# Delta-rule attention and an MLP on one core: join products on four 32x32 tiles, state updates with 48 stationary columns, and another planned order

## The chip, the cores and the metric

The kernel runs on one core of a Trainium2 chip. The metric is the time of one execution on the device in microseconds (us); lower is better. TensorE (PE in the profile) multiplies, VectorE (DVE), ScalarE (ACT) and GpSimd (POOL) work element by element, and SyncE (SP) issues most of the transfers.

## The reference

Two blocks follow each other, all in float32. The first is a linear attention with the delta rule: 4 x 8 heads, 768 tokens, 48 values a head, and a state of 48x48 for each head.

```python
k_n = k / (np.linalg.norm(k, axis=-1, keepdims=True) + 1e-06)
state = np.zeros((B, H, D, D))
for t in range(S):
    y[:, :, t] = q[:, :, t] @ state                       # before the update
    v_old = state^T k_n[t]
    state = state + beta[t] * outer(k_n[t], v[t] - v_old)
```

The result is laid out as (4, 768, 384) and goes through a layer norm and an MLP with a residual:

```python
xn = (x - mean) / sqrt(var + 1e-6) * g_ln
out = x + relu(xn @ w_ch1) @ w_ch2                        # 384 -> 1536 -> 384
```

## The kernel before

**Tiling.** The tokens are worked in 12 chunks of 64 (C), all 32 heads of a chunk at once. Two chunks form a slab. The step by step recurrence within a chunk is replaced by the inverse of a triangular matrix of 64x64 for each head, X, built from the gram matrix of the keys. Its two diagonal blocks of 32 rows (BK) come from `rows_inverse`: for a slab, 31 rows, each with a product (L1051, into tmp) and a subtraction (L1058, into xb) on VectorE, every one of which depends on the one before. The blocks then go through memory (xb to xd to xt). The block below the diagonal is made by `join` from two groups of products: e = gram block times the first diagonal block (L1118), then z = the second diagonal block times e (L1123). Each group has 32 products of 32x32, for 16 heads in each of two partition halves. `blocks_join` does the same a level lower, for chunk 1 alone, whose inverse is built from blocks of 16.

**One chunk on TensorE** then takes these small groups of 32 products each, named here as in the prediction: the gram matrices (L967, kt only), P (queries times keys, L967 with qt), e and z (the join), ks (state times keys, L1168 into two), qs (state times queries, L1168 into by), u (L1223), y (L1230, the chunk's output) and the state update s (L1240). Between them stand other engines: v minus ks on VectorE (L1175), the copy of u on ScalarE (L1225), s added to s_all on VectorE (L1250), the masked P on VectorE (L998), and for the join a transpose on VectorE (L1111) and evictions on ScalarE (L1128 into es, L1133 into xt). A small product is placed in the array by the partitions of its operands: the rows by where they are read, the columns by where the output lies. `quad(n)` is the n-th strip of 32 partitions, `half(n)` the n-th of 64.

**The MLP** works on the 256 tokens that a chunk has over the 4 batches. Chunks 0 to 2 have a plain first layer (L1495), the others one with eleven products instead of twelve (L1428); the second layer is plain for chunk 0 (L1517) and has seven products instead of eight for the others (L1596). It reads its normed input xnt some way behind y: copy, statistics, scaling, transposing, partly through memory.

**The order.** The code does not fix the order by itself. Each step (a group of products, one element-wise operation, one transfer) is handed to `Line.add` with an assumed cost, its dependencies and a priority. `Line.schedule` runs a planner: it works backwards from due times, then forwards with the assumed costs, and picks for each engine what starts next. The steps are then emitted in order of planned start, and every engine executes its own list in that order, transfers of SP and ACT in one common order. So a step that waits holds all that stands behind it on its engine. The numbers that steer the planner are HOP (time from a step to a dependent one on another engine), 0.03 us for a dependent step on the same engine, PASS (a small product's half, 0.0165 us), the lists DUE and CAP (due times of the MLPs and of single steps), and URGENT (how far a small group may go ahead of MLP work). Where TensorE would wait long, the planner inserts products of zeros (L1674) that keep its clock up.

Of the kernel before, what the change touches and what calls it, by code (L numbers as in the profile page):

```python
# [74 lines left out]
class Line:  # L75
# [3 lines left out]
    HOP, GIVE, PATIENCE, SLACK, EAGER = 0.17, 0.1, 0.8, 3.0, 0.068  # L79
# [132 lines left out]
    def offer(self, u):  # L212
        t = u.t0
        for d in u.deps:
            t = max(t, d.end + (0.03 if d.eng == u.eng and d.bulk is None else self.HOP))
        u.ready = t + u.lag
        self.avail[u.eng].append((u.ready, u))

    def foresee(self, now):

        soon, ends = {e: [] for e in ENGS}, {}
        for s in self.held:
# [5 lines left out]
            for d in s.deps:  # L228
                z = d.end if d.end is not None else ends.get(d, max(now, self.free[d.eng]) + d.cost)
                t = max(t, z + (0.03 if d.eng == s.eng and d.bulk is None else self.HOP))  # L230
# [129 lines left out]
    def schedule(self):  # L360
# [5 lines left out]
        for s in reversed(every):  # L366
            took = s.cost if s.bulk is None else s.cost + self.DMA_ISSUE + self.DMA_DONE + 2 * s.bulk
            took = max(took, 0.031 * s.np if s.due is None else 0.0)
            late = [u.pr - took - (0.03 if u.eng == s.eng else self.HOP) for u in users[s]]
# [32 lines left out]
def kernel(  # L402
# [129 lines left out]
    ATT = FK[2]  # L532
    hp_e = ((0, 0), (1, 1), (0, 1), (1, 0))
# [223 lines left out]
    def pe(n, fn, r, w, arr=0.0, **kw):  # L757
        return add("PE", n * PASS, fn, r, w, np=n, arr=arr, **kw)
# [312 lines left out]
    def blocks_join(c, **kw):  # L1071
# [5 lines left out]
        XN, ES = ([(n, 0), (n, 1)] for n in ("xn", "es"))  # L1077
# [14 lines left out]
        pe(128, prod_e, gk + XN, ATT, 0.22, **kw)  # L1092
        add("ACT", act(512), lambda: nc.scalar.mul(es, pe_, -1.0), ATT, ES, **kw)
        pe(128, prod_z, ES + xq + XT, BY[:2], 0.22, **kw)
# [6 lines left out]
    def xt_keys(c):  # L1101
        return [("xq", c % NX, n) for n in range(8)] + [("xz", c % NX)] + [
            (n, c % NX, g) for n in ("xt", "xo") for g in range(2)
        ]

    def join(c, **kw):
# [8 lines left out]
        def prod_e():  # L1115
            for h in range(GH):
                for e in range(2):
                    nc.tensor.matmul(p[quad(2 * e + 1), h], gs[quad(2 * e), h, BK:C], xnj[quad(2 * e), h])  # L1118

        def prod_z():  # L1120
            for h in range(GH):
                for e in range(2):
                    nc.tensor.matmul(p[quad(2 * e), h], es[quad(2 * e + 1), h], xt[quad(2 * e + 1), h, c0 : c0 + BK])  # L1123

        pe(64, prod_e, gk + [("xn", 0), ("xn", 1)], [ATT[1]], 0.11, name=f"e{c}", **kw)
        for e in range(2):
            rows = quad(2 * e + 1)
            add("ACT", act(512), lambda rows=rows: nc.scalar.mul(es[rows], p[rows], -1.0), [ATT[1]], [("es", e)], **kw)  # L1128
        pe(64, prod_z, [("es", 0), ("es", 1)] + xq, [ATT[0]], 0.11, name=f"z{c}", **kw)
        for e in range(2):  # L1130
            rows = quad(2 * e)
            add(
# [684 lines left out]
```

## Time and profile before

| | us |
|---|---|
| median of 3 runs | 560.88 |
| runs | 559.5 to 561.1 |
| span of the profiled execution | 559.2 |
| TensorE busy in it | 527.6 |
| VectorE busy | 365.0 |
| GpSimd busy | 252.5 |
| ScalarE busy | 193.1 |

The profiled execution has its span as its own time, from the first to the last instruction; what the device time has around it is not in the trace, and the median of the runs lies 1.7 us above that span. An engine's busy time does not hold the issue of transfers. TensorE's matmuls overlap, so groups of them are compared from their start to the next start.

### The profile page before, as it was taken

How to read it: one execution, taken by the hardware profiler on the slowest of the kernel's cores; microseconds unless marked ns; L12 is line 12 of the kernel's file. 1: busy time of each engine (PE TensorE's matmuls, PEld its weight loads, DVE VectorE, ACT ScalarE, POOL GpSimd, SP SyncE). 2: the span in 40 equal slices, each digit the busy share in tenths (PEclk: the TensorE clock that was granted, in tenths of full speed). 3: DMA queues.
4: the chain of work that ended last, by engine and by line, in shares of the span. 5: the costliest groups of instructions: out<-in, count | busy, mean ns of one | idle time of the engine just before them, and what ended most of it. 6: DMA issues, size and time to landing. Idle time of an engine off the chain costs nothing. (4 is left out here: it accounts for less than half of the span.)

```text
span 559.2 us, 23067 instructions
## 1 busy us (share of the span) xinstructions
PE 527.6 (94%) x10052; PEld 479.9 (86%) x10052; DVE 365.0 (65%) x884; ACT 193.1 (35%) x452; POOL 252.5 (45%) x399
## 2 busy tenths in 40 slices
PE   7778979999959999999999998999999999999996
PEld 4667857689848899998999988999999999999996
DVE  6775459870898833898957886758979336253331
ACT  5786733232222324322403314404412225323030
POOL 5362428319863565375363314361353602426243
PEclk9897989999989999999999999999999999999999
DMA  9884883579344677544525255652523410111101
GB/s 170 277 156 127 210 207 53 83 195 119 64 74 65 153 161 98 108 87 96 112 52 91 46 111 111 133 111 58 115 38 83 106 30 32 31 35 53 28 1 29
DMA packets 195973, 54.67 MB, mean 98 GB/s; under 512 B 186136, under 2 KB 189344, under 8 KB 195872
## 3 DMA queue, kind: packets, MB, share of 16 engines
q1 hardware_dynamic: 190112, 40.39, 37.4%
q10 hardware_dynamic: 3552, 9.63, 5.3%
q0 software_dynamic: 2208, 3.17, 3.6%
q8 instruction: 79, 1.29, 1.0%
q14 instruction: 22, 0.18, 0.1%
HBM read 36.38 MB, written 16.78 MB: 95 GB/s over the span
## 5 line engine op out<-in xcount | busy, mean ns | idle before, releaser
L1596 PE MATMUL f<-w_sb,h_all 128*128 128x192 f32 x396 | 95.0, 330 | 0.0
L1582 POOL TENSOR_TENSOR h_all<-h_all 128x256 f32<-128x256 f32 x99 | 72.9, 739 | 48.2 <-PE f L1596 41.9
L1596 PE MATMUL f<-words,h_all 128*128 128x192 f32 x396 | 91.2, 329 | 0.1
L1428 PE MATMUL f<-xnt,w_sb 128*128 128x128 f32 x648 | 89.2, 277 | 0.0
L1621 POOL TENSOR_TENSOR words<-h_all 128x128 f32<-128x128 f32 x66 | 30.4, 473 | 123.6 <-ACT h_all L1447 105.3
L1428 PEld LDWEIGHTS f<-xnt,w_sb 128*128 128x128 f32 x648 | 81.0, 192 | 0.8
L1450 DVE TENSOR_TENSOR h_all<-f,h_all 128x256 f32<-128x256 f32 x135 | 56.4, 420 | 34.6 <-PE f L1428 22.9
L1058 DVE TENSOR_TENSOR xb<-xb,tmp 128x60 f32<-128x60 f32 (+19 forms) x170 | 71.8, 423 | 3.3
L1051 DVE TENSOR_TENSOR tmp<-xb,gb 128x60 f32<-128x60 f32 (+19 forms) x170 | 68.8, 405 | 3.8 <-DVE gb L1041 0.5
L1596 PEld LDWEIGHTS f<-words,h_all 128*128 128x128 f32 x396 | 67.9, 190 | 0.9 <-issue 0.2
L1596 PEld LDWEIGHTS f<-w_sb,h_all 128*128 128x128 f32 x396 | 66.4, 190 | 1.2 <-issue 0.2
L1495 PE MATMUL f<-xnt,w_sb 128*128 128x256 f32 x216 | 52.3, 394 | 2.6 <-ACT h_all L1504 2.6
L1495 PEld LDWEIGHTS f<-xnt,w_sb 128*128 128x128 f32 x216 | 41.0, 195 | 10.6 <-ACT h_all L1504 3.5
L559 POOL DMA_DIRECT2D tb<-in_k_dram x64 | 42.0, 661 | 11.8 <-DVE kt L947 11.4
L1614 DVE TENSOR_TENSOR o<-f,x 128x192 f32<-128x192 f32 x33 | 11.7, 355 | 53.2 <-PE f L1596 42.5
L1447 ACT ACTIVATE h_all<-f 128x256 f32<-128x256 f32 x54 | 20.6, 382 | 55.8 <-PE f L1428 33.7
L1596 PE MATMUL f<-w_sb,words 128*128 128x192 f32 x132 | 32.8, 332 | 1.2 <-DVE o L1614 1.2
L1504 ACT ACTIVATE h_all<-f 128x256 f32<-128x256 f32 x36 | 13.6, 381 | 40.2 <-PE f L1495 32.5
L1447 ACT ACTIVATE h_all<-h_all 128x256 f32<-128x256 f32 x54 | 22.1, 413 | 12.8 <-DVE h_all L1450 12.5
L1614 POOL TENSOR_TENSOR o<-o,words 128x192 f32<-128x192 f32 x22 | 13.1, 613 | 25.9 <-DVE words L1614 25.9
L1596 PEld LDWEIGHTS f<-w_sb,words 128*128 128x128 f32 x132 | 22.5, 190 | 1.8 <-DVE o L1614 1.5
L1444 ACT COPY h_all<-f 128x256 f32<-128x256 f32 x27 | 10.0, 372 | 36.9 <-PE f L1428 36.8
(235 smaller groups left out, 936.5 us busy)
## 6 DMA issues: line engine op xcount, KB each, us to landing
words<-in_moe_w_ch_dram ACTq DMA_DIRECT2D x10, 768.0 KB, 5.5
gd<-gsb SPq DMA_DIRECT2D x11, 512.0 KB, 4.9
v<-in_v_dram SPq DMA_DIRECT2D x24, 192.0 KB, 3.6
out_dram<-o SPq DMA_DIRECT2D x48, 96.0 KB, 2.3
kr<-in_k_dram SPq DMA_DIRECT2D x46, 96.0 KB, 3.1
xld<-xlt SPq DMA_DIRECT2D x9, 384.0 KB, 2.6
xnt<-xld SPq DMA_DIRECT2D x36, 96.0 KB, 2.7
gb<-gd SPq DMA_DIRECT2D x40, 64.0 KB, 3.1
```

The source lines that it names most:

```text
L559: add(eng, cost, lambda: QUEUE[eng].dma_start(out=out_, in_=in_), r, w, bulk=n * ns / 16e3, **kw)
L1051: lambda j=j, n=n, w=w, t=t: nc.vector.tensor_tensor(out=t, in0=xv[:, 0:n, j : j + 1].to_broadcast([128, n, w]), in1=gv[:, j : j + 1, j + ...
L1058: "DVE", dve(n * w), lambda t=t, rest=rest: nc.vector.tensor_tensor(out=rest, in0=rest, in1=t, op=ALU.subtract),
L1428: nc.tensor.matmul(wide(p[:, 128 * n : 128 * n + 128]), w[:, f : f + 128], r, start=start and n == 0, stop=stop, skip_group_check=True)
L1447: add("ACT", act(256), lambda: nc.scalar.activation(to[0], p, ACTF.Relu), pk, to[1])
L1450: add("DVE", dve(256), lambda: nc.vector.tensor_tensor(out=to[0], in0=ps(p), in1=y[0], op=op), [*pk, *y[1]], to[1])
L1495: nc.tensor.matmul(p[:, 0:TOK], w1_sb[:, t, f * 128 : (f + 1) * 128], xnt[:, t], start=(t == 0), stop=(t == KC - 1))
L1504: lambda hk=hk, p=p: nc.scalar.activation(h_all[:, hk] if c <= LNPE else h_all[:, hk].rearrange("p (g i b) -> p i g b", g=2, b=BK), p[:, 0 ...
L1582: add(eng, cost, lambda: e.tensor_tensor(out=out_, in0=x, in1=y, op=op), r, w, port=2 if eng == "Pool" else 1, pr=-2)
L1596: lambda f=f, t=start and f == 0: nc.tensor.matmul(p[:, 0:D2], lhs(f), rhs[:, f], start=t, stop=(f == F2 - 1), skip_group_check=True),
L1614: lambda: e.tensor_tensor(out=out_, in0=a, in1=b_, op=ALU.add), r, w, pr=pr,
L1621: lambda f=f + i: e.tensor_tensor(out=s3[f], in0=one(0, 0)[0](f), in1=one(1, 0)[0](f), op=ALU.subtract),
```

## The change

- In `join`, the 32 products of e and of z are placed on four 32x32 tiles in turn instead of two: heads of even and odd number now write different column strips. They read the same two row strips as before. Each eviction of 32 partitions x 512 elements becomes two of 32 x 256, one for each parity of head.
- In `state_up`, the stationary side has 48 columns (D) instead of 64 (DP, of which 16 are zeros) in all chunks but the first. s_all is written in 112 partitions instead of 128.
- In the planner, join products, the products of `blocks_join` and state updates have lower assumed costs (0.0097 and 0.0135 us for half a product), a dependent step of the same engine may start at once (NEXT = 0.0 instead of 0.03), and DUE, CAP and with them URGENT have other values. The planned order of all engines differs in consequence. The same 5,059 products are issued on TensorE, 22 of them products of zeros as before.

```diff
-    HOP, GIVE, PATIENCE, SLACK, EAGER = 0.17, 0.1, 0.8, 3.0, 0.068
+    HOP, NEXT, GIVE, PATIENCE, SLACK, EAGER = 0.17, 0.0, 0.1, 0.8, 3.0, 0.068
...
-            t = max(t, d.end + (0.03 if d.eng == u.eng and d.bulk is None else self.HOP))
+            t = max(t, d.end + (self.NEXT if d.eng == u.eng and d.bulk is None else self.HOP))
...
+    SROWS = slice(0, DP + D)
...
-    def pe(n, fn, r, w, arr=0.0, **kw):
-        return add("PE", n * PASS, fn, r, w, np=n, arr=arr, **kw)
+    def pe(n, fn, r, w, arr=0.0, per=PASS, **kw):
+        return add("PE", n * per, fn, r, w, np=n, arr=arr, **kw)
...
         def prod_e():
-            for h in range(GH):
-                for e in range(2):
-                    nc.tensor.matmul(p[quad(2 * e + 1), h], gs[quad(2 * e), h, BK:C], xnj[quad(2 * e), h])
+            for j in range(GP):
+                for hp, e in hp_e:
+                    h = 2 * j + hp
+                    nc.tensor.matmul(p[quad(2 * e + 1 - hp), h], gs[quad(2 * e), h, BK:C], xnj[quad(2 * e), h])
 
         def prod_z():
-            for h in range(GH):
-                for e in range(2):
-                    nc.tensor.matmul(p[quad(2 * e), h], es[quad(2 * e + 1), h], xt[quad(2 * e + 1), h, c0 : c0 + BK])
...
+            for j in range(GP):
+                for hp, e in hp_e:
+                    h = 2 * j + hp
+                    nc.tensor.matmul(p[quad(2 * e + hp), h], es[quad(2 * e + 1), h], xt[quad(2 * e + 1), h, c0 : c0 + BK])
+
+        pe(64, prod_e, gk + [("xn", 0), ("xn", 1)], ATT, 0.11, per=0.0097, name=f"e{c}", **kw)
+        for hp, e in hp_e:
+            o, i = es[quad(2 * e + 1), hp::2], p[quad(2 * e + 1 - hp), hp::2]
+            add("ACT", act(256), lambda o=o, i=i: nc.scalar.mul(o, i, -1.0), ATT, [("es", e, hp)], **kw)
...
         def state_up():
-            p_s = p_2
+            p_s, w = p_2, D if c else DP
...
-                        p_s[half(hp), e, j], kp[half(e ^ hp), h0 * DP : h0 * DP + DP], us[half(e ^ hp), h0]
+                        p_s[DP * hp : DP * hp + w, e, j], kp[half(e ^ hp), h0 * DP : h0 * DP + w], us[half(e ^ hp), h0]
...
-                add("DVE", dve(768), lambda: nc.vector.tensor_tensor(out=s_all, in0=s_all, in1=p_2, op=ALU.add), TWO, ["s_all"], **kw)
+                add("DVE", dve(768), lambda: nc.vector.tensor_tensor(out=s_all[SROWS], in0=s_all[SROWS], in1=p_2[SROWS], op=ALU.add), TWO, ["s_all"], **kw)
...
-    DUE = [48.277, 71.818, 105.201, 129.927, 160.904, 198.354, 225.618, 268.079, 296.41, 349.475, 397.211, 414.674, 2.36, 1.205, 1.444, 27.102]
-    CAP = [80.445, 120.608, 203.575, 297.613, 389.16, 84.616, 102.629, 154.396, 189.571, 211.797, 265.167, 306.93, 344.143, 373.749, 426.77]
+    DUE = [50.992, 114.068, 314.926, 205.564, 149.356, 477.876, 478.934, 312.28, 346.185, 350.453, 686.787, 470.901, 1.129, 0.014, 0.752, 73.348]
+    CAP = [205.235, 241.575, 287.664, 628.512, 352.468, 284.041, 97.509, 453.871, 237.917, 199.779, 306.658, 413.158, 502.3, 617.624, 487.101]
```

33 lines of the change are left out of this document (13 added, 20 removed).

## The prediction

> **What bounds the kernel now.** I read the page first (busy times, slices, chain), then the busy times by stretch, then the order of events on TensorE and VectorE in the stretch that is not full. Times are us from the start of the span. A product shows as two records, so a group of 32 small products is "x64".
>
> ```profile
> span 559.2 us, 23067 instructions
> ...
> PE 527.6 (94%) x10052; PEld 479.9 (86%) x10052; DVE 365.0 (65%) x884; ACT 193.1 (35%) x452; POOL 252.5 (45%) x399
> ...
> PEclk9897989999989999999999999999999999999999
> ...
> PE 39%; ACT 0%; DVE 0%; issue 0%; DVEq 0%
> ```
>
> TensorE is busy for 94%, the chain that ended last consists of TensorE work alone for its last 39% (217 us), and the granted clock is full but for a few early slices. The next view, busy time of each engine by stretch, tells where the other 32 us are.
>
> ```profile
> core 0: us, PE busy (x) PEld busy (x) DVE busy (x) ACT busy (x) POOL busy (x), PEclk, DMA share, GB/s
> ...
> 60.00:100.00 40.00, 35.87 (x834) 27.32 (x836) 26.91 (x56) 17.29 (x31) 22.76 (x28) 0.96 0.63 133
> ...
> 150.00:175.00 25.00, 18.27 (x515) 15.34 (x508) 23.27 (x39) 7.71 (x19) 13.19 (x17) 0.86 0.51 79
> 175.00:555.00 380.00, 375.98 (x6769) 357.94 (x6767) 244.81 (x586) 113.68 (x276) 164.91 (x272) 1.00 0.38 78
> ```
>
> From 175 on TensorE is busy for 376 of 380 us: there each us of TensorE work taken away is a us of the time. From 150 to 175 it is busy for 18.3 of 25 us at clock 0.86, and part of that is products of zeros that only keep the clock up. So there are two places for a gain: less TensorE work after 175, and an order that has no hole before it.
>
> **The two new product shapes.** TensorE's events in order of time; the columns are start, length, engine, line, shapes, count:
>
> ```profile
> 79.00 1.29 PE L1085 MATMUL f<-xnj,gsb 32*32 32x32 f32 x128
> 80.21 1.56 PE L1495 MATMUL f<-xnt,w_sb 128*128 128x256 f32 x6
> ...
> 376.30 1.20 PE L1118 MATMUL by<-xnj,gsb 32*32 32x32 f32 x64
> 377.43 0.59 PE L1596 MATMUL f<-w_sb,h_all 128*128 128x192 f32 x2
> ...
> 391.81 1.11 PE L1240 MATMUL two<-u,kr 64*64 64x48 f32 x64
> 392.85 1.16 PE L1428 MATMUL f<-xnt,w_sb 128*128 128x128 f32 x8
> ```
>
> From start to the next start, a join product on two 32x32 tiles takes 1.13 us for 64 passes, and blocks_join on four tiles 1.21 us for 128. About 0.1 us of each is the change to and from another shape (my estimate: the difference between a lone small group and one that follows another). So a pass costs 16 ns on two tiles and 8.7 on four, 32 to 35 ns for each tile either way: what counts is how many tiles take turns. On four tiles a join product should cost 64 x 8.7 ns + 0.1 = 0.66 us and save 0.47. Bounds: 0.52, if the whole 1.21 halves, and nothing, if four tiles that share two row strips do not overlap as the four of blocks_join do, which lie in four row strips. I take 0.47, because the state update (four tiles on two row strips, 64 stationary columns) runs at (1.04 - 0.1) / 64 = 14.7 ns a pass, 29 ns for each strip, less than the 32 ns that a strip takes now for half the columns; a strip that served one tile at a time could not do that. There are 22 such products (11 chunks, two each), 16 of them after 175: 7.5 us there.
>
> A rule of the Trainium skill speaks against this edit: "TensorE: Matmul & The Clock Gate", Part 3 (Packing small matmuls), says that a weight load overlaps running products only where the row group differs. By it the join products would stay at 1.13 us, since the row strips are two before and after. The state update's 29 ns speaks against the rule here, but in another tile size, so it is a rival below.
>
> The state update loads 48 stationary columns in place of 64. The weight loads by column count, and the evictions that change, from the groups of instructions:
>
> ```profile
> L1428 PEld LDWEIGHTS f<-xnt,w_sb 128*128 128x128 f32 x648 | 81.0, 192 | 0.8
> ...
> L1240 PEld LDWEIGHTS two<-u,kr 64*64 64x64 f32 x704 | 11.7, 135 | 2.0 <-issue 1.9
> ...
> L1118 PEld LDWEIGHTS by<-xnj,gsb 32*32 32x32 f32 x384 | 6.5, 108 | 0.9 <-ACT rstd L1280 0.2 <-issue 0.2
> ...
> L1128 ACT ACTIVATE es<-by 32x512 f32<-32x512 f32 x12 | 7.1, 589 | 16.1 <-PE by L1118 16.0
> ...
> L877 ACT COPY xt<-by 64x256 f32<-64x256 f32 (+1 forms) x9 | 3.3, 366 | 0.8 <-ACT h_all L742 0.7
> ```
>
> The load grows by 0.85 ns a column (108, 135, 192), and a tile's pass is 32 ns at 32 columns and 59 at 64, so I put 48 columns at the middle, 45.5: 16 x 45.5 ns + 0.1 = 0.83 us instead of 1.04, 0.21 saved (between nothing, if the 48 moving columns set the pace, and 0.26, if it falls in proportion). Ten updates, eight after 175: 1.7 us. With the joins 9.2 us after 175.
>
> What it adds: each join eviction becomes four of 32x256 for two of 32x512, 4 x 366 - 2 x 589 = 0.29 us more ScalarE for each product, 6.4 us on an engine that is busy for 35%. On the path it lengthens product to product by 0.29 us; in the changed order at least 3 us of TensorE work stand between e and z and between z and u, against about 1.7 needed, so I cost it at nothing. The 48 rows of s_all change no element count.
>
> **The order.** The planner's smaller step between dependents, its new due times and costs give another order from the start. TensorE, VectorE and SyncE around the hole:
>
> ```profile
> 95.04 0.68 PE L1187 MATMUL two<-v,xt 32*64 32x48 f32 x32
> ...
> 99.34 1.15 PE L1230 MATMUL by<-u,pt 64*64 64x48 f32 x64
> ...
> 105.33 3.39 PE L1517 MATMUL f<-w_sb,h_all 128*128 128x384 f32 x10
> ...
> 122.94 10.63 PE L1495 MATMUL f<-xnt,w_sb 128*128 128x256 f32 x48
> ...
> 146.78 1.20 PE L1118 MATMUL f<-xnj,gsb 32*32 32x32 f32 x64
> ...
> 165.09 1.99 PE L967 MATMUL two<-qt,kt 48*64 48x64 f32 x64 [5.05 <-DVE s_all L1250]
> 167.01 3.87 PE L1674 MATMUL f<-u 128*128 128x256 f32 x10
> ...
> 181.91 1.15 PE L1230 MATMUL by<-u,pt 64*64 64x48 f32 x64
> ```
>
> ```profile
> 85.91 0.71 DVE L1111 STREAM_TRANSPOSE xnj<-xt 128x512 f32<-128x512 f32 x1
> ...
> 122.23 0.21 DVE L1058 TENSOR_TENSOR xb<-xb,tmp 128x31 f32<-128x31 f32 x1
> ...
> 138.04 0.36 DVE L1614 TENSOR_TENSOR o<-f,x 128x192 f32<-128x192 f32 x1 [13.94 <-PE f L1596]
> ...
> 145.33 0.70 DVE L1111 STREAM_TRANSPOSE xnj<-xt 128x512 f32<-128x512 f32 x1
> ...
> 154.83 2.11 DVE L1058 TENSOR_TENSOR xb<-xb,tmp 128x192 f32<-128x192 f32 x1
> ...
> 162.05 1.24 DVE L947 STREAM_TRANSPOSE qt<-tb 128x1024 f32<-128x1024 f32 x1
> ...
> 164.09 0.95 DVE L1250 TENSOR_TENSOR s_all<-s_all,two 128x768 f32<-128x768 f32 x1
> ```
>
> ```profile
> 61.23 4.79 SPq L559 DMA_DIRECT2D gb<-gd  x6
> ...
> 66.73 6.71 SPq L559 DMA_DIRECT2D xt<-xd  x8
> ```
>
> ```profile
> L1058 DVE TENSOR_TENSOR xb<-xb,tmp 128x60 f32<-128x60 f32 (+19 forms) x170 | 71.8, 423 | 3.3
> ```
>
> ```profile
> 541.27 13.54 PE f L1596 x82
> ```
>
> Now the row inverse of chunks 2 and 3 (62 dependent VectorE steps, two for each row) is done at 122.4, but chunk 2's join transpose comes only at 145.33, because on VectorE an eviction of the MLP stands ahead of it and waits 13.94 us for TensorE. TensorE uses up the MLP of chunks 0 and 1 meanwhile, and when chunks 2 and 3 start at 146.78 there is nothing left to lie beside them: the hole from 150 to 175.
>
> In the changed program VectorE has, behind chunk 1's join transpose, 41 of those 62 steps, chunk 1's subtraction from v, the other 20, then kt, s_all, kt; the join transpose of chunk 2 stands ahead of every MLP eviction. TensorE's order keeps MLP work back: 12 second-layer products (24 passes), all 36 first-layer products of chunk 1 and 36 of the 42 of its second layer (the sevens, L1596) lie among the steps of chunks 2 and 3. Worked out:
> - The small inverse for chunk 1 runs without a break and its eight reads (6.71 us of issue) no longer stand behind six gb reads (4.79 us) and what lies around them, so chunk 1's join transpose comes near 76 instead of 86. Then 41 x 0.42 (the mean step, stalls included) = 17 and 0.95 for v: its u products start at 94.5, as now (95.0). They now wait for those 41 steps; until then TensorE has MLP work of chunk 0 beside the join.
> - y of chunk 1 starts near 98.6 and ends at 99.7. Then 20 steps, kt 1.24 and s_all 0.95 must end before the next gram: 95.5 + 8.4 + 2.2 = 106.1. TensorE has no other work there: 6.5 us lost, 1 more between the two grams. This is the place of the old hole's remainder.
> - From there to y of chunk 3: second layer 24 x 0.339 = 8.1, first layer 72 x 0.221 = 15.9, sevens 72 x 0.165 = 11.9, fourteen small groups at 1.06 = 14.8, four join products at 0.66 = 2.6, two transposes 1.7: 55.0. With 7.5 lost and 3 for waits that the trace of before can't show, y of chunk 3 starts at 98.6 + 65.5 = 164.1, against 181.91: 17.8 earlier.
> - Of this 7.3 is owed: at that point 12 first-layer products (24 x 0.221) and 6 sevens (12 x 0.165) are still to do that are done now. Net 10.5.
>
> After it each chunk's MLP starts at least 26 us of TensorE work behind its y (20 now), u stands 2.6 us or more behind ks and y 2.6 or more behind u, which need 1.2 and 1.0: TensorE stays full as now. After the last y 55 us of MLP work are left, 66 now; both are more than the last chunk's way to its MLP. Head and tail don't change.
>
> **The sum.** 559.2 - 9.2 - 10.5 = 539.5 for the span. The profiled span lies 1.7 under the median of the runs (560.88), so 541.2; I say 541.
>
> **The rivals.**
> - Two row strips don't overlap: 20 join products on the full stretches save nothing, 0.47 x 20 = 9.4 more: 550. For it, the rule above; against it, the state update's 29 ns. Chance 0.12.
> - The hole only moves: VectorE, busy 23.3 of 25 us in the hole, is the true limit until 175, and y of chunk 3 comes just the 7.3 us earlier that are owed. Then only the work after 175 goes: 559.2 - 9.2 + 1.7 = 552. For it, VectorE's share; against it, the 13.94 us that it sat waiting just before. Chance 0.16.
> - Slower: the 61 steps in a row hold v, kt and s_all of all else, and run at their disturbed length. A step beside GpSimd work took 2.11 us at 154.83, where the mean is 0.42, and in the changed order v's scaling, twelve DMA issues and weight conversions on GpSimd lie beside them. At 1 us a step they end 61 x 0.58 = 35 us later, nothing on TensorE covers it, and the clock falls: 541 + 35 = 576. It decides from 0.42 + 19.7 / 61 = 0.74 us a step. Against it, the mean over 170 steps of 0.42, which has such stalls in it. Chance 0.08.
> - The narrower stationary side does nothing, because the moving columns set the pace: 541 + 2 = 543. Chance 0.04.
>
> **How the numbers follow.** The forecast keeps 0.60. A difference of 0.3% (1.7 us) is what measurement can tell here. Faster: the forecast, three of the rivals, less a little for the hole moving the wrong way: 0.91; within 0.3%: 0.01; slower: 0.08. The range: 532 if no unseen wait comes up and the 7.5 us are mostly filled; the upper end takes in the two rivals at 550 and 552 with 3 us of unseen waits, 555. Outside lie the slow case and some of either side.
>
> **What would show it.** Join groups near 0.66 us and state updates near 0.83 from start to next start; TensorE busy for all but about 8 us between 95 and 165, with the idle time put down to VectorE's kt or s_all; y of chunk 3 near 164; no zeros behind it. Join groups at 1.1 would show the strip rule, a y of chunk 3 behind 175 the moved hole, and steps at L1051 and L1058 of 0.7 us or more on average the slow case.

## The result, and the profile after

Five runs of each kernel beside each other: before 561.1 us (559.5 to 563.8), after 554.18 us (553.1 to 557.3), a ratio of 0.9895 with the 95% interval 0.9857 to 0.9934. The forecast was 541. The direction is right, the gain is 1.05% where 3.5% was forecast. The profiled execution took 553.6 us, its span 551.7. Some executions of a kernel run in a slower state; ratios leave these out here and below, medians do not.

The page of the kernel after, the same lines as before; line numbers from 560 to 1150 are one to three higher than before (1118 became 1120, 1123 became 1126, 1051 and 1058 became 1052 and 1059, 967 became 968).

```profile
span 551.7 us, 23098 instructions
...
PE 513.7 (93%) x10052; PEld 466.8 (85%) x10052; DVE 380.2 (69%) x884; ACT 198.8 (36%) x496; POOL 255.6 (46%) x399
...
PEclk9898989999797899999999999999999999999999
...
PE 81%; DVE 6%; DMA 4%; issue 3%; ACT 2%; SPq 2%; POOL 0%; ACTq 0%; DVEq 0%; POOLq 0%
```

TensorE is busy for 13.9 us less (527.6 before), but the span is only 7.5 shorter: 6.4 us of idle time came in. The granted clock has the digits 7, 9, 7 and 8 between 138 and 193. The busy times by stretch (PE, PEld, DVE, ACT, POOL, then the clock, the DMA share and GB/s):

```profile
150.00:175.00 25.00, 20.36 (x469) 18.81 (x467) 19.97 (x26) 4.02 (x13) 21.67 (x30) 0.95 0.44 73
175.00:548.00 373.00, 367.03 (x6522) 349.92 (x6522) 251.32 (x581) 116.21 (x306) 165.01 (x271) 0.99 0.38 78
```

The stretch 150 to 175 still lacks 4.6 us, and after 175 there are now 6 us of idle time in 373, where there were 4 in 380. TensorE's events in order show where; first the two new shapes, then two places at which it stands still:

```profile
119.97 0.75 PE L1120 MATMUL f<-xnj,gsb 32*32 32x32 f32 x64
120.65 1.15 PE L1168 MATMUL by<-s_all,qt 48*64 48x48 f32 x64
...
133.83 0.94 PE L1240 MATMUL two<-u,kr 64*48 64x48 f32 x64
134.58 1.13 PE L1230 MATMUL by<-u,pt 64*64 64x48 f32 x64
135.64 0.73 PE L1126 MATMUL f<-xt,es 32*32 32x32 f32 x61
138.95 0.31 PE L1126 MATMUL f<-xt,es 32*32 32x32 f32 x3 [2.58 <-issue]
139.19 11.00 PE L1495 MATMUL f<-xnt,w_sb 128*128 128x256 f32 x36
...
168.07 1.11 PE L1230 MATMUL by<-u,pt 64*64 64x48 f32 x64
...
176.00 1.99 PE L968 MATMUL two<-kt 48*64 48x64 f32 x64 [5.64 <-DVE s_all L1250]
...
180.00 4.13 PE L1495 MATMUL f<-xnt,w_sb 128*128 128x256 f32 x12
```

A join product takes 0.68 us from start to start (1.13 before), a state update 0.75 (1.04 before). Then, in the middle of chunk 3's second join product, 2.58 us in which TensorE waits for nothing that the profile shows, and behind it 36 records that take 11.0 us where 48 took 10.63 before: the granted clock was half (0.5) from 138.4 to 145.2. And right behind the y of chunk 3 a hole: the next gram waits 5.64 us for s_all, and runs at half clock itself (172.5 to 182.8). VectorE and GpSimd beside this hole:

```profile
166.19 0.42 DVE L1052 TENSOR_TENSOR tmp<-xb,gb 128x247 f32<-128x247 f32 x1
166.64 0.82 DVE L1059 TENSOR_TENSOR xb<-xb,tmp 128x247 f32<-128x247 f32 x1
167.50 2.77 DVE L1052 TENSOR_TENSOR tmp<-xb,gb 128x240 f32<-128x240 f32 x1
170.30 3.68 DVE L1059 TENSOR_TENSOR xb<-xb,tmp 128x240 f32<-128x240 f32 x1
...
175.01 0.94 DVE L1250 TENSOR_TENSOR s_all<-s_all,two 112x768 f32<-112x768 f32 x1
```

```profile
167.33 0.74 POOL L1582 TENSOR_TENSOR h_all<-h_all 128x256 f32<-128x256 f32 x1
168.02 0.60 POOL L1614 TENSOR_TENSOR o<-o,x 128x192 f32<-128x192 f32 x1
168.57 1.00 POOL L1384 TENSOR_TENSOR q_last<-w_sb 128x384 f32<-128x384 f32 x1
...
170.81 1.94 POOL L1384 TENSOR_TENSOR qt<-w_sb 128x384 f32<-128x384 f32 x2
172.71 2.11 POOL L1384 TENSOR_TENSOR pt<-w_sb 128x384 f32<-128x384 f32 x2
```

Two steps of the row inverse of chunks 4 and 5 take 2.77 and 3.68 us, in the same microseconds in which GpSimd adds blocks of first-layer weights (L1384, the function sums_of_w1), beside the first step right behind two additions of another sort (L1582, L1614). Such a step alone takes 0.42 (166.19); the one right ahead of the two takes 0.82. s_all stands behind them in VectorE's order, and the gram waits for s_all.

### The profile page after: what moved, and what is told of

Same layout as the page of the kernel before. It is cut to its first block, busy times and chain, and to the rows that moved or that the text cites. A ratio compares the mean times of both kernels' runs of the same rounds, so it can differ in the third digit from the quotient of the medians.

```text
span 551.7 us, 23098 instructions
## 1 busy us (share of the span) xinstructions
PE 513.7 (93%) x10052; PEld 466.8 (85%) x10052; DVE 380.2 (69%) x884; ACT 198.8 (36%) x496; POOL 255.6 (46%) x399
## 4 chain that ended last, share of the span: by engine, by line
PE 81%; DVE 6%; DMA 4%; issue 3%; ACT 2%; SPq 2%; POOL 0%; ACTq 0%; DVEq 0%; POOLq 0%
PE f L1596 26%; PE f L1428 25%; PE f L1495 9%; PE two L968 4%; PE f L1517 3%; PE by L1230 2%; PE by L1168 2%; PE two L1223 2%; PE two L1168 2%; DVE xb L1059 2%; SPq L560 2%; DVE tmp L1052 2%; DMA tb<-in_k_dram 1%; PE two L1240 1%; DMA words<-in_moe_w_ch_dram 1%
## 5 line engine op out<-in xcount | busy, mean ns | idle before, releaser
L1596 PE MATMUL f<-w_sb,h_all 128*128 128x192 f32 x396 | 97.6, 333 | 0.0
L1582 POOL TENSOR_TENSOR h_all<-h_all 128x256 f32<-128x256 f32 x99 | 73.5, 749 | 51.3 <-PE f L1596 38.4
L1596 PE MATMUL f<-words,h_all 128*128 128x192 f32 x396 | 87.7, 330 | 0.0
L1428 PE MATMUL f<-xnt,w_sb 128*128 128x128 f32 x648 | 87.3, 277 | 0.0
L1428 PEld LDWEIGHTS f<-xnt,w_sb 128*128 128x128 f32 x648 | 80.0, 192 | 0.5
L1450 DVE TENSOR_TENSOR h_all<-f,h_all 128x256 f32<-128x256 f32 x135 | 55.7, 422 | 32.3 <-PE f L1428 23.7
L1052 DVE TENSOR_TENSOR tmp<-xb,gb 128x60 f32<-128x60 f32 (+19 forms) x170 | 70.3, 413 | 5.8 <-POOL xb L1039 1.1
L1059 DVE TENSOR_TENSOR xb<-xb,tmp 128x60 f32<-128x60 f32 (+19 forms) x170 | 69.1, 407 | 4.8
L1495 PE MATMUL f<-xnt,w_sb 128*128 128x256 f32 x216 | 55.2, 414 | 0.0
L1495 PEld LDWEIGHTS f<-xnt,w_sb 128*128 128x128 f32 x216 | 44.0, 208 | 7.3
L1614 DVE TENSOR_TENSOR o<-f,x 128x192 f32<-128x192 f32 x33 | 11.6, 351 | 45.9 <-PE f L1596 25.5
L1268 ACT COPY x<-by 128x384 f32<-128x384 f32 x23 | 10.4, 480 | 45.0 <-DVE o L1614 18.8
L1614 POOL TENSOR_TENSOR o<-o,words 128x192 f32<-128x192 f32 x22 | 13.1, 617 | 24.5 <-DVE words L1614 20.3
```

The source lines that it names most:

```text
L1052: lambda j=j, n=n, w=w, t=t: nc.vector.tensor_tensor(out=t, in0=xv[:, 0:n, j : j + 1].to_broadcast([128, n, w]), in1=gv[:, j : j + 1, j + ...
L1059: "DVE", dve(n * w), lambda t=t, rest=rest: nc.vector.tensor_tensor(out=rest, in0=rest, in1=t, op=ALU.subtract),
L1428: nc.tensor.matmul(wide(p[:, 128 * n : 128 * n + 128]), w[:, f : f + 128], r, start=start and n == 0, stop=stop, skip_group_check=True)
L1450: add("DVE", dve(256), lambda: nc.vector.tensor_tensor(out=to[0], in0=ps(p), in1=y[0], op=op), [*pk, *y[1]], to[1])
L1495: nc.tensor.matmul(p[:, 0:TOK], w1_sb[:, t, f * 128 : (f + 1) * 128], xnt[:, t], start=(t == 0), stop=(t == KC - 1))
L1582: add(eng, cost, lambda: e.tensor_tensor(out=out_, in0=x, in1=y, op=op), r, w, port=2 if eng == "Pool" else 1, pr=-2)
```

## The experiments

Each kernel was run beside the kernel before on its chip. The expectations number their theories: from e4 on, theory 1 is that the hole comes from two row-inverse steps that GpSimd's sums hold up, theory 2 that TensorE stands without instructions, theory 3 that ScalarE's order in the head costs time; e1 to e3 have a theory 1 of their own. An edit moves a kernel's line numbers: in e3 the lines behind 1130 are ten higher than in the kernel before (1250 is the state update), in e7 three higher than in the kernel after (1243). The last two columns are from its profiled execution: the start of chunk 3's y, and the time from there to the end of the last product (the forecast for the kernel after: 164.1, and 554.80 - 181.91 = 372.9 less the 9.2 of the shapes plus 7.3 owed = 371.0).

| kernel | median us | ratio to before, 95% interval | y of chunk 3 | from it to the last product |
|---|---|---|---|---|
| before | 561.1 | 1 | 181.9 | 372.9 |
| after | 554.18 | 0.9895 (0.9857 to 0.9934) | 168.1 | 378.7 |
| e1: joins on two tiles | 561.97 | 0.9982 (0.9950 to 1.0014) | 171.2 | 383.2 |
| e2: 64 columns | 555.72 | 0.9911 (0.9873 to 0.9949) | 168.0 | 379.1 |
| e3: shapes, old planner numbers | 559.56 | 0.9966 (0.9936 to 0.9995) | 178.9 | 371.5 |
| e4: fills for the sums | 545.40 | 0.9696 (0.9650 to 0.9742) | 163.5 | 370.9 |
| e5: sums on VectorE, at once | 551.10 | 0.9830 (0.9776 to 0.9884) | 169.7 | 374.9 |
| e6: sums later on GpSimd | 553.69 | 0.9887 (0.9836 to 0.9937) | 168.3 | 380.3 |
| e7: 32 tiny products at the head | 560.26, one run | | 175.4 | 378.2 |
| e8: copies for the sums | 547.21, one run | | 168.4 | 372.1 |
| e9: sums on VectorE, behind evictions | 546.74 | 0.9775 (0.9740 to 0.9809) | 171.7 | 370.9 |
| e10: two roots moved | 558.02 | 0.9955 (0.9926 to 0.9983) | 173.4 | 378.6 |
| e11: e9 and e10 | 553.19 | 0.9884 (0.9853 to 0.9915) | 169.8 | 375.9 |
| e12: e11 and the join product moved | 546.31 | 0.9750 (0.9709 to 0.9792) | 168.1 | 372.5 |
| e13: e9 and the join product moved | 547.80 | 0.9756 (0.9717 to 0.9794) | 165.1 | 371.8 |
| e14: the join product moved, alone | 551.31 | 0.9799 (0.9751 to 0.9847) | 165.8 | 379.0 |
| e15: e13 and the first root moved | 544.02 | 0.9710 (0.9668 to 0.9751) | 164.6 | 372.1 |

**e1 and e2: what the shapes are worth in the new order.** Each undoes one shape and leaves the order of all engines alone.

```
e1  -  p[quad(2 * e + 1 - hp), h]      (prod_e)      -  p[quad(2 * e + hp), h]     (prod_z)
    +  p[quad(2 * e + 1), h]                         +  p[quad(2 * e), h]
e2  -  p_s, w = p_2, D if c else DP
    +  p_s, w = p_2, DP
```

> The changed kernel, in its own order, with the products of the joins back on two of the four 32x32 tiles; nothing else differs. Theory 1 (a join product on four tiles saves 0.47 us, and it lies on TensorE's path): 16 of the 22 products come after 175 us, so 7.5 us at least and 10.3 if all count: 554.2 becomes 562 to 564.5, and each product shows about 1.13 us in the trace where the changed kernel has 0.66. Rival (TensorE waits elsewhere, the products' length is not on the path): within 2 us of 554.

> The changed kernel, in its own order, with 64 stationary columns in the state update of every chunk. Theory 1 (the product takes 0.75 to 0.83 us with 48 columns and 1.04 with 64, on TensorE's path): 8 of them cost 0.21 to 0.29 each, 1.7 to 2.3 us: 555.9 to 556.5. Rival (off the path): 554.2.

With the joins on two tiles the gain is gone: 0.9982, the span 559.4 where the kernel after has 551.7. A join record comes every 16.0 ns in it and every 8.9 ns in the kernel after. So the joins lie on the path, as theory 1 has it, but the loss is smaller than it said: 0.0087 of the time, 4.9 us, where it had 7.5 at least. The traces show 4.5 us more behind chunk 3's y (383.2 for 378.7), with 3.4 us less of half clock there (6.8 for 10.2) and 0.9 us less of a stop at the next state update (1.07 for 1.98). The 64 columns cost 0.0016 of the time, 0.9 us, as expected in sign, but within the intervals; a record of the state update between small groups comes every 14.8 ns, with 48 columns every 11.6.

**e3: the shapes without the new planning numbers.** The kernel before with the two new shapes; NEXT, DUE, CAP and the costs as they were. The joins' evictions now depend on both halves of their bank, so some steps move even so.

> The kernel before with the four-tile joins and the 48-column state update, and the planner's numbers as they were before (the dependences of the joins on both halves of their bank, which four tiles need, move some steps behind chunk 3). Theory 1 (the shapes save 9.2 us after 175, the new order's gain before 175 is eaten by the hole at 170 to 184): 561.1 - 9.2 = about 552, no slower than the changed kernel. Rival (the shapes bring their saving only because the new order has work for TensorE to take up): 558 to 561, slower than the changed kernel by 4 or more.

559.56, a gain of 0.34% alone: the rival is right. The shapes save no more than 1.4 us from chunk 3's y to the end (371.5 for 372.9), though every join and update has its new length. TensorE's events show what took the saving back, above all this:

```profile
216.71 1.15 PE L1240 MATMUL by<-u,pt 64*64 64x48 f32 x64
217.68 0.45 PE L1250 MATMUL two<-u,kr 64*48 64x48 f32 x24
221.06 1.05 PE L1250 MATMUL two<-u,kr 64*48 64x48 f32 x40 [2.93 <-issue]
222.05 1.01 PE L1606 MATMUL f<-w_sb,words 128*128 128x192 f32 x2
```

After a join product and a y the state update stops at its record 24 for 2.93 us, again put down to "issue", and the next product takes 1.01 us for a usual 0.59: the clock was half from 221.1 to 224.5, and once more from 320.0 to 323.5, behind a stop of 1.48 us. All stops of TensorE of over 0.3 us behind chunk 3's y add up to 8.0 us in e3, 5.9 of them put down to issue, and to 3.3 in the kernel before. With 3.4 us for the 6.8 us at half clock that is 8.1 us, about the 7.8 that the forecast's 9.2 lacks (my sum from these rows; which of the stops the shapes made is not shown).

**e4 and e8: who holds the two row-inverse steps.** GpSimd's six sums become fills that read nothing (e4), or copies that read one operand (e8); both leave the sums out, so what the kernel computes from them is not computed.

```
-  nc.gpsimd.tensor_tensor(out=o[:, f], in0=a[:, f], in1=b[:, f], op=op)
+  nc.gpsimd.memset(o[:, f], 0.0)                       # e4
+  nc.gpsimd.tensor_copy(out=o[:, f], in_=a[:, f])      # e8
```

> The changed kernel, in its own order, with GpSimd's six sums of first-layer weights at 150 to 175 us replaced by fills of the same slices with zero, which read nothing (their values, and what is computed from them, are left out). Theory 1 (the two steps of the row inverse that took 2.77 and 3.68 us stood behind these sums, and that opened TensorE's hole at 170 to 184): the steps go back to about 0.4 us, the hole and the half clock behind it go, 8 us less: about 546. By the Trainium skill (SBUF — State Buffer, on the port pair that VectorE and GpSimd share), a GpSimd instruction that reads no SBUF does not lock out a VectorE instruction with two SBUF inputs; that would let the steps go free. Rival A (the steps are slow from something else, or a fill locks VectorE as well): the hole stays, 553 to 554.5. Rival B (the hole goes but the time is taken up by the next late thing): 550 or more.

> The changed kernel, in its own order, with the six sums replaced by GpSimd copies of one operand each (the other operand, and with it the right values, are left out). It tells whether GpSimd's reading of SBUF at all holds up VectorE's steps with two inputs, or its second operand. Theory 1 with the rule of the Trainium skill (SBUF — State Buffer): a GpSimd instruction that reads SBUF locks the shared ports for all its length, so the two row-inverse steps stay long, above 1.5 us, and most of the hole stays. Rival (two operands on GpSimd are needed for it): the steps fall to about 0.4 us and the hole goes, as with the fills.

The fills close the hole: 545.4 us. The same two steps, s_all and the next gram in e4 (VectorE, then TensorE):

```profile
162.28 1.07 DVE L1052 TENSOR_TENSOR tmp<-xb,gb 128x240 f32<-128x240 f32 x1
163.38 0.68 DVE L1059 TENSOR_TENSOR xb<-xb,tmp 128x240 f32<-128x240 f32 x1
...
164.56 0.94 DVE L1250 TENSOR_TENSOR s_all<-s_all,two 112x768 f32<-112x768 f32 x1
```

```profile
163.50 1.11 PE L1230 MATMUL by<-u,pt 64*64 64x48 f32 x64
...
165.71 1.16 PE L968 MATMUL two<-kt 48*64 48x64 f32 x64
```

6.45 us for the two have become 1.75 (two additions of another sort, at L1582 and L1614, still lie beside them), s_all comes 1.06 us after y's start instead of 6.94, and TensorE is busy for 25.00 of the 25 us from 150 to 175. From y to the last product it takes 370.9 us, the forecast's 371.0, and 7.8 less than in the kernel after. By the ratios e4 gains 11 us on the kernel after; the 3 us beyond the hole are not explained (y of chunk 3 came 4.6 us earlier in its profile).

The copies of e8 go another way than my theory said. They read SBUF, and yet the second step is short, those beside the copies take 0.57 us, not 1.5 or more, and the gram waits 1.20 us for s_all, not 5.64:

```profile
167.37 2.18 DVE L1052 TENSOR_TENSOR tmp<-xb,gb 128x240 f32<-128x240 f32 x1
169.59 0.59 DVE L1059 TENSOR_TENSOR xb<-xb,tmp 128x240 f32<-128x240 f32 x1
...
172.22 0.57 DVE L1052 TENSOR_TENSOR tmp<-xb,gb 128x220 f32<-128x220 f32 x1
```

```profile
167.28 0.73 POOL L1582 TENSOR_TENSOR h_all<-h_all 128x256 f32<-128x256 f32 x1
167.96 0.60 POOL L1614 TENSOR_TENSOR o<-o,x 128x192 f32<-128x192 f32 x1
168.49 0.50 POOL L1384 COPY q_last<-w_sb 128x384 f32<-128x384 f32 x1
...
171.32 1.83 POOL L1384 COPY pt<-w_sb 128x384 f32<-128x384 f32 x2
```

The 2.18 us are those beside two GpSimd additions and a copy that follow each other at once; beside copies alone both sides slow (a step 0.57 for 0.39, a copy 0.9 for 0.5). By the Trainium skill ("SBUF — State Buffer", section "SBUF: two separate sides") a VectorE instruction with two SBUF inputs is locked out for the whole of a GpSimd instruction that reads SBUF. The fills agree with it. The additions agree in kind, though the step of 3.68 us in the kernel after waited for three of them in a row. The copies agree at most in part: the step that starts at 172.82 ends at 173.39, though the copy beside it lasts until 173.15 and such a step alone takes 0.39.

**e5, e6, e9: the sums at another place.** All three compute them. In e5 they are on VectorE right behind chunk 3's s_all, in e9 on VectorE behind the two evictions of the second layer that follow, in e6 five of them stay on GpSimd behind two additions to o. The lists of all other instructions are unchanged; the edit sets the planned start by which steps are emitted (in e9 the number 164.2 stands there):

```
+  for i, s in enumerate(s for s in line.steps if s.name == "w1sum"):
+      s.start = <the step named above>.start + 1e-4 * (i + 1)
```

> The changed kernel with the six sums of first-layer weights on VectorE, right behind chunk 3's addition to s_all, instead of on GpSimd; the orders of TensorE, ScalarE and SyncE and the rest of VectorE's are as they were. Theory 1 (the hole at 170 to 184 is nothing but two row-inverse steps that GpSimd's sums hold up): the steps take about 0.4 us, the hole goes, and VectorE's 3 us for the sums come after what TensorE waits for: about 546, as with the fills that read nothing. Rival (VectorE is full there anyway, so work moved onto it makes the next gram as late): 552 to 554.

> The changed kernel with five of the six sums of first-layer weights still on GpSimd, but behind two additions to o that wait for TensorE's second layer, some 10 us later; all other orders as they were. Theory 1: they still hold up row-inverse steps, but behind chunk 3's s_all, where nothing waits for these steps: the hole at 170 to 184 goes, about 546 to 548. Rival (GpSimd's later work, 5 us behind, now makes the second layer's operands late): 550 to 556.

> The changed kernel with the six sums of first-layer weights on VectorE, now behind the two additions to o and v2 that free banks of the second layer (in the kernel with the sums right behind s_all, TensorE waited 2.7 us for one of these); all other orders as they were. Theory 1: neither the next gram nor a bank waits for the sums; from y of chunk 3 to the last product it takes 371 us as with the fills (370.9), not 378.7: 554.2 - 8 = 546. Rival (the three us of sums on VectorE show up at another place): 549 to 552.

e5 gains about half, 0.983: the gram no longer waits, but a product of the first layer waits 2.73 us for the eviction that now stands behind the sums. e9 puts them behind it and reaches 0.9775, by the ratios 6.7 us less than the kernel after, with 370.9 us from y to the end: what theory 1 said for that stretch. e6 gains nothing, 0.9887, though the hole at 170 is gone: without a sum right behind L1582 and L1614 the two steps take 0.86 and 0.68 us, and the gram waits 0.20. It shows best what the wait is. The first line of each view stands beside the five moved sums, the others 8 us later (VectorE, then GpSimd):

```profile
176.19 1.02 DVE L1059 TENSOR_TENSOR xb<-xb,tmp 128x175 f32<-128x175 f32 x1
...
184.61 6.58 DVE L1059 TENSOR_TENSOR xb<-xb,tmp 128x60 f32<-128x60 f32 x1
```

```profile
175.92 2.15 POOL L1384 TENSOR_TENSOR qt<-w_sb 128x384 f32<-128x384 f32 x2
...
184.79 0.88 POOL L1621 TENSOR_TENSOR words<-h_all 128x128 f32<-128x128 f32 x2
185.62 0.99 POOL L1384 TENSOR_TENSOR w_sb<-w_sb 128x384 f32<-128x384 f32 x1
...
189.72 1.40 POOL L1582 TENSOR_TENSOR h_all<-h_all 128x256 f32<-128x256 f32 x2
191.08 0.99 POOL L1384 TENSOR_TENSOR w_sb<-w_sb 128x384 f32<-128x384 f32 x1
```

```profile
199.72 1.98 PE L968 MATMUL two<-qt,kt 48*64 48x64 f32 x64 [4.99 <-DVE qt L948]
```

GpSimd, 5 us behind now, has no pause between its additions from 184.8 on, and a VectorE step that takes 0.22 us elsewhere (60 elements a partition, at 102.4 in the kernel after) takes 6.58, until 191.2. It waited not for one instruction but for a row of them. That is not always so: the five steps beside the five moved sums took 0.98 to 1.02 us each, about one sum, and in the kernel before, beside the same sums, steps of 1.02, 2.11 and 1.05 stand between 152.6 and 158.0. What decides between one and a row is not shown. The hole is 4.99 us again, only later, at the transpose of the next chunk's queries: the row inverse ends at 193.5, SyncE holds the transfer of xb until then and issues the load of the queries behind it, and the transpose waits 2.96 us for that load. The rival named the time, 550 to 556, but had GpSimd late for TensorE; it was VectorE, late behind GpSimd, and a load late behind VectorE.

**e7, e12, e13, e14: the idle time called issue.** e7 shifts TensorE's whole instruction stream by half a block, with 32 tiny products at its head. e12 to e14 move chunk 3's second join product, with its evictions, behind two groups of first-layer products; e14 does only that.

> The changed kernel, in its own order, with 32 tiny products (64 matmul records, 128 TensorE instructions) added at its head, so that each instruction of TensorE lies half of a 16 KB block of 256 instructions further on. Theory 2 (the idle times put down to issue, 2.2 us in blocks_join's first product and 2.6 us at record 61 of chunk 3's last join product, are TensorE out of instructions, at the end of a block of 256): the second moves 64 records back, to about record 61 of the y group ahead of that join product, about as long; and the first moves 64 records back as well. Rival (it waits there for an operand or a bank): it stays at record 61 of the join product. The time: within 3 us of 554.

> The changed kernel with chunk 3's second join product behind two groups of first-layer products and nothing else; GpSimd's sums stay where they were. Theory 2: the 2.6 us of idle time at it go, and the half clock of 138 to 145 behind it: 2 to 5 us, 549 to 552. Rival (what is gained there is lost again at the next gram, which waits for VectorE's s_all behind GpSimd's sums at a fixed time): 553.5 to 554.5.

> The sums on VectorE behind the evictions, and chunk 3's second join product behind two groups of first-layer products; the roots as the changed kernel has them. Theories 1 and 2 together: 546.7 - 3 to 4 = about 543, with no idle time at that product and the y of chunk 3 at 164 to 168; the forecast of 541 would then have failed by these two stalls and little else. Rival (the gain of the moved product came from the moved roots): 546 to 547.

> As the kernel with both, and chunk 3's second join product moved behind two groups of first-layer products, with its evictions. Theory 2 (s, y and this product in a row use up TensorE's instructions faster than blocks of 256 come in; 2.0 to 2.8 us of idle time at it in each run of this order): with large products between them the block is there in time, the wait goes, 2 us less than the kernel with both, and more where the half clock behind it goes as well. Rival (the wait is for its operand or bank, or moves on to the next small group): no difference within 1 us.

In e7 (one run of 560.26 us, above the 557 expected at most; its head was slow, with y of chunk 0 at 55.7) the same row of small groups runs through without a stop:

```profile
146.95 0.94 PE L1243 MATMUL two<-u,kr 64*48 64x48 f32 x64
147.70 1.11 PE L1233 MATMUL by<-u,pt 64*64 64x48 f32 x64
148.75 0.75 PE L1129 MATMUL f<-xt,es 32*32 32x32 f32 x64
149.43 4.80 PE L1498 MATMUL f<-xnt,w_sb 128*128 128x256 f32 x21
```

The operands, banks and order are the same, so the rival, that the product waits for one of these, falls. The stop did not move 64 records back, as I had expected, but away: other places have one now (2.5 and 2.4 us in the first inverse, 1.5 us in a qs product at 131). What stays is where in the count of instructions it happens. Numbering TensorE's loads and products in order of time, in the kernel after the stops of over 1 us called issue come at numbers 2985, 3749, 6047 and 8853; modulo 256 that is 169, 165, 159 and 149. In e7 they come at 696, 1713 and 5283: 184, 177 and 163. The place creeps as instructions of other kinds add up. Counted with those, TensorE's waits and other instructions of its sequencer, it does not creep at all: every stop of over 1 us called issue, 59 of them in the 17 traces of this case, the kernel before among them, begins at number 193 modulo 256 (counted from 0). The page of the kernel after has the transfers:

```profile
q8 instruction: 78, 1.28, 1.0%
```

78 packets of 16.4 KB for 20,104 loads and products, 258 to a packet. In the trace of the kernel after no two of these packets start within 3.5 us of each other. 256 instructions are 128 records, which a join runs through in 128 x 8.9 ns = 1.1 us. Where small groups follow each other, TensorE is through its block before the next is there: each of the four stops ends 1.4 to 1.9 us behind the end of one of these packets, with no other between. The Trainium skill ("Runtime: NRT & Kernel Launch", section "Instruction fetch mechanics") has the blocks of 16 KiB and 256 instructions, and the trace agrees; it also says that their fetching is hidden, because instructions are issued more slowly than the blocks come. Here, with 8.9 ns a record, it is not: 2.58 us in one place.

Moved alone (e14) the join product gains 0.0096 of the time against the kernel after, 5.4 us; the intervals do not meet. y of chunk 3 comes at 165.8 although y of chunk 1 came 2.5 us later than in the kernel after (106.15 for 103.68), and the wait at that product is 0.66 us. Against e11 it gains 7.5 us (e12), clear of the intervals and more than the stop explains: in the profiles 2.9 us of it lie between y of chunk 1 and y of chunk 3, and 3.4 behind. On top of e9 (e13) it gains 1 us of the 3 to 4 expected, not to be told from nothing: there the two do not add up in the time, though y of chunk 3 in the profile, 165.1, is 6.5 us earlier than in e9 (3.7 of it from an earlier y of chunk 0). That is not settled. From chunk 2's gram to y of chunk 3 the profiles have 56.0 to 56.6 us in the four kernels with the product moved, and 57.9 to 61.4 in eight that have the same products there unmoved; the 61.4 is the kernel after.

**e10, e11, e15: the head.** In the new order a square root on ScalarE stands ahead of copies that TensorE needs, and its data is late (ScalarE, then TensorE, kernel after):

```profile
41.45 0.23 ACT L1031 ACTIVATE nrm_b<-gb 128x16 f32<-128x16 f32 x1 [4.71 <-DMA tb<-in_k_dram]
41.59 1.14 ACT L878 COPY xt<-by 128x256 f32<-128x256 f32 x3
```

```profile
42.77 1.14 PE L920 MATMUL by<-qt,gsb 64*64 64x64 f32 x32 [3.98 <-ACT xt L878]
```

> The changed kernel with two square roots of the row inverses on ScalarE (they wait for a load: 4.7 us at 37 and 2.6 us at 70) moved behind the copies that TensorE waits for, and VectorE's steps that use them behind the predicated copies and the join transpose; GpSimd's sums stay where they hurt. Theory 3 (the new order loses 4 us at 38.8 to 42.8 because ScalarE's xt copies stand behind a root whose data is not there yet, and 0 to 6 us, different in each execution, at the first product of blocks_join's second half): y of chunk 0 at about 48 where it is 51.6, y of chunk 1 two to four us earlier, 550 to 552. Rival (the loads themselves set chunk 1's way, TensorE only waits at another place): 553.5 to 554.5.

> The sums on VectorE behind the evictions and the two roots behind the copies, together. Theories 1 and 3 add up: 546 - 3 = about 543, close to the forecast of 541 for the changed kernel. If theory 3 falls: 546. If the gains eat each other: 548 or more.

> As the kernel with the sums and the moved product, and only the first of the two square roots (chunk 1's small inverse) behind ScalarE's copies, VectorE's five steps that use it behind the predicated copy. Theory 3, narrowed after its first form lost (the root of chunks 2 and 3, moved, pushed all their row steps and with them v back by 4 us): the first root alone makes y of chunk 0 come 3 to 4 us earlier and costs nothing later, so 0 to 3 us less than the kernel with the sums and the moved product. Rival (chunk 1's loads set the way to its join, so nothing before it counts): no difference within 1 us.

Theory 3 falls in its first form. With both roots moved the wait at 42.77 is gone and y of chunk 0 comes at 49.8 for 51.6, but y of chunk 1 comes at 108.9 for 103.7, and the time is 558.0. The row inverse of chunks 2 and 3 starts later, and v of chunk 1 stands behind 41 of its steps:

```profile
PE two L1187 <- DVE v L1175: 3.5, 1, 3.5
```

(TensorE waits for VectorE; us in total, times, longest.) e11 is worse than e9 by 0.0109. Its profile has the same wait for v (3.1 us), but also 5.0 us more behind chunk 3's y (375.9 for 370.9), with a wait of 1.98 us for a join's eviction at 213.1 and 6.8 us of half clock behind that; how much each costs is not shown. With the first root alone moved (e15) y of chunk 0 comes at 47.3 and the time is the best of all, 544.0, 0.971 of before; against e13 that is 2.6 us, expected 0 to 3, and not clear of the intervals. Against the kernel before (0.9668 to 0.9751) and the kernel after (0.9857 to 0.9934) it is clear.

## Why the prediction missed, step by step

- **Joins: right.** 0.66 us forecast, 0.68 measured, 8.9 ns a record for 8.7. The rival with the rule of the Trainium skill ("TensorE: Matmul & The Clock Gate", Part 3), that only another row group lets loads overlap, does not hold for these products: two row strips carry four tiles at the rate of blocks_join's four strips. e1 shows that it lies on the path.
- **State update: right.** 0.83 forecast; measured 0.83 ahead of a large product, as the 1.04 before was taken, and 0.75 between small groups. e2's 0.9 us is too small to be told.
- **9.2 us after chunk 3's y: right as a sum, hidden by the next point.** Where the hole is closed (e4, e9) the last stretch is 370.9 us, forecast 371.0.
- **"TensorE stays full as now" behind y of chunk 3: this step failed, and cost 8 of the 13 us** (7.8 in the trace, 6.7 in the time of e9). I counted TensorE's work between dependent steps, and priced VectorE's steps with their mean. The mean held: 0.41 and 0.41 us over 170 each, 0.41 and 0.42 before. But two of 340 steps were 2.77 and 3.68 us long, and they stood ahead of s_all, for which the next gram waits. My slower rival had the mechanism, a row-inverse step beside GpSimd, and had looked for it at chunks 2 and 3 and for the steps' mean; it came at chunks 4 and 5, in two steps. The row that I quoted for it (2.11 us at 154.83 before) had been beside the same sums.
- **y of chunk 3 at 164.1: 4.0 us late; the terms that failed are the waits.** u of chunk 1 was to start at 94.5, "as now", and started at 98.1: the head did change, by the root ahead of the copies (4.0 us) and 2.2 us of missing instructions in blocks_join. But this delay hardly reaches chunk 3. Chunk 2's gram, forecast for 106.1, started at 106.66, because TensorE lost about 2 us ahead of it, filled with products of zeros, where I had 6.5. (My 106.1 starts from 95.5, though the terms ahead of it, 76, 17 and 0.95, end at 94.0.) The other 3.4 us came between this gram and y of chunk 3: 61.4 us for a forecast of 58.0. There stand the 2.6 us without instructions and 6.8 us of half clock behind them, for which the sum had only 3 us of unnamed waits. With the join product moved (e14) this stretch takes 56.6 us. That the head came out near the forecast is in part luck: in the profiles of the eight kernels that are the same up to there (after, e4, e5, e6, e8, e9, e13 and e14), chunk 2's gram starts between 105.6 and 113.5.
- **The evictions in four pieces: right.** In the kernel after no wait for an eviction of a join is among TensorE's waits of 0.2 us and more (e11 has one of 1.98 us).
- **The sum.** 541 + 8 for the hole + 4 before y of chunk 3 = 553; measured 554.2. The range's upper end of 555, made of the rivals at 550 and 552, just held it. The rival that the hole only moves gave 552, close in number and wrong in kind: y of chunk 3 came 13.8 us earlier, not 7.3, and the loss came behind it.

What neither the forecast nor a rival had is the supply of instructions. The kernel's own planner has it: it counts passes in blocks and lets none begin within 3.95 us of the last (`BLOCK, FIRST, FETCH = 128, 93, 3.95`), and puts small groups where that costs least. That fits e3, which keeps the old costs for the new shapes and gains 0.34% where the kernel after gains 1.05%: the new costs and due times are a part of the change's worth, not a by-product of the shapes. That e3 loses for this reason alone is argued from its stops and the two stretches of half clock, not shown.

Still open: why e13 gains so little over e9; and how much of the spread of these kernels (up to 8 us between executions of one) is the head, where TensorE's wait for ScalarE's copies was 2.4 us in e4's profiled execution and 8.2 in e9's.

## What to carry to other kernels

A mean over many steps says nothing about the one step that something waits for: list what stands ahead of the awaited instruction on its own engine, and what GpSimd does in those microseconds. Moving two-operand GpSimd work along VectorE's two-operand steps can move the wait with it, as in e6; look where GpSimd would run without a pause. And when small products get shorter, count instructions as well as cycles: no two blocks came within 3.5 us here, 14 ns for each of 256 instructions (an estimate from the packets of the kernel after), and a join at 8.9 ns a record takes 4.5 ns an instruction. What several such groups gain in a row can go into waiting for the next block, unless large products stand between.

## What the runs showed of the hardware

- A VectorE step with two SBUF operands beside GpSimd additions waited for about one of them (0.98 to 1.02 us, five steps in e6) or for a row of them: 3.68 us in the kernel after, 6.58 us in e6. Beside GpSimd fills it took 0.4, as alone, beside GpSimd copies 0.57.
- TensorE's instructions come in packets of 16.4 KB, none within 3.5 us of the last in the kernel after, and small products outrun them: waits of 1.4 to 2.6 us. All 59 such stops of over 1 us in 17 traces begin at instruction 193 modulo 256 of TensorE's list.
- Half clock stood behind stops, though not behind each: the stop in chunk 3's second join product, 2.0 to 2.6 us long in ten kernels, was followed by 3.4 or 6.8 us of it in seven (6.8 in the kernel after), and the hole of 5.64 us by 10.2 (172.5 to 182.8). So a stop can cost more than its length: 12 records of the first layer took 4.13 us at 180.0, and 2.96 in e9.
- Four 32x32 tiles on two row strips run at 8.9 ns a record, two tiles at 16.0.
